# Chunked attention and a routed expert layer in one kernel: each batch's three slots in two phases, routing by batch

## The chip, the cores and the metric

The kernel runs on one core of one Trainium2 chip. The core has TensorE (matrix products and transposes; PE, with its weight loads as PEld), VectorE (DVE), ScalarE (ACT), GpSimd (POOL) and SyncE (SP), each with its own queue of instructions, and 16 DMA engines that all queues share. SBUF is the working memory with 128 partitions; PSUM is the memory that TensorE writes, in eight banks. The metric is the device time of one execution in microseconds (us), taken as the median of several runs. The profile is of one execution of its own.

## The reference

The input is four batches, eight heads, 768 positions and 64 values a head. Attention is by chunks of 32 queries: a chunk sees 8 memory keys, its own 32 positions, 16 to the left and 8 to the right, so 64 keys. Its output, 3072 tokens of 512 values, goes into a layer of 8 experts, two for each token, chosen by noisy logits.

```python
for c in range(nc):                                  # 24 chunks of 32 queries
    k_full = np.concatenate([mem_k, k_ctx], axis=2)  # 8 + up to 56 keys
    scores = scale * np.matmul(q_c, k_full.transpose(0, 1, 3, 2))
    a = np.exp(scores - np.max(scores, axis=-1, keepdims=True))
    a = a / (np.sum(a, axis=-1, keepdims=True) + 1e-09)
    out[:, :, c_start:c_end] = np.matmul(a, v_full)

logits = x @ w_gate
noisy_logits = logits + np.log1p(np.exp(x @ w_noise)) * noise
top2 = np.argpartition(-noisy_logits, 2, axis=1)[:, :2]
# top2_w: softmax over the two chosen logits
for e in range(E):
    for k in range(2):
        mask = top2[:, k] == e
        h = np.maximum(x[mask] @ w1[e], 0.0)
        out[mask] += top2_w[mask, k, None] * (h @ w2[e])
```

## The kernel before

**Two stages.** First attention with routing, then the experts. A token's pair of experts is one of 28; attention's rows are written to a DRAM table `xd`, and routing makes for each pair a list of up to 128 tokens, so that the expert stage gathers 128 rows of a pair at a time (L671), multiplies them by both experts' weights (L714, L726) and scatters the result (L677). The first gather needs all of routing.

**Slots.** A batch has 768 tokens: three slots (`TP` = 3) of 256, twelve slots (`NT`) in all. A slot goes through these steps, each a function:
- `scores` (L402): 40 small matmuls into PSUM `ps_s`, then on VectorE the row maximum (L423) and the subtraction into `sc` (L425).
- `exps` (L428): ScalarE's exponential into `pb`.
- `turn_p` (L433): eight 128x128 turns on TensorE into a PSUM bank, copied by ScalarE into `pT`.
- `values` (L442): row sums (L447) and products with the windows of v (L453) on TensorE into `ps_o`; on VectorE the reciprocals (L457) and two scalings (L460) into `xrow`.
- `turn_x` (L466): turns of the rows, copied by ScalarE into `xT`.
- `gate` (L475): logits of eight experts and eight noise columns, copied by VectorE into `lg_all`.

Ahead of a batch's first scores stand its `turns` (L546, `turn` L387): eight units, four of k and four of q, each with twelve turns on TensorE and two copies (k, L398) or one (q, L397). The turned keys are held once (`kT`), the turned queries twice (`qT`).

**Loads.** The inputs of a batch come by POOL's queue (`load_v`, `load_kq`, into two buffers `nat`), with a cast to bf16. POOL spreads v by heads (`spread_v`, L368); SP's queue writes it to DRAM, and POOL's queue reads it back in windows (`window_v`, L374 to L383) into one of two buffers `vb`. All of this, and the buffers of `xrow`, lies in the SBUF space of the weights of experts 2 to 7 (experts 0 and 1 hold none but small inputs), so the weights are loaded late: experts 0, 1 and 2 by `load_expert` in batch 2, the others during the expert stage.

**Routing.** `Route` holds a run of token groups of 128. Its steps are `noise` (two ScalarE operations, L247 and L248), `choose` (14 VectorE operations, L265 to L282, ending in the one-hot `ohp` of the pair), `weights` and `values` (POOL or VectorE), `order`, `ranks` (TensorE, L288 to L292), `settle` (VectorE, L317 to L335: ranks, totals, one-hot slots), `lists` (TensorE, L352, and an addition, L359), and at the end `decode` into gather indices (L490 to L498).

**What sets the order.** Under `manual_schedule` (L516) the program's order is the order on TensorE, ScalarE, VectorE and SP; on POOL the pinned instructions keep theirs. The loop over slots (L562) is a pipeline: in step i it issues the scores of slot i+1, the turns of slot i's probabilities, the row turns of slot i-1, the values of slot i, the exponentials of slot i+1 and the logits of slot i-1. The turns of the next batch stand in the middle slot of a batch (`PLAN`, L558; half of batch 2's and 3's query units one step earlier than the rest). Of k and q, q is loaded and turned first from batch 1 on. Routing is in four runs (L561): `r0` of 6 groups, `ra` of 8, `rb` of 6 and `rc` of 4, whose steps are spread over later slots; `rb` and `rc` are interleaved after the last slot (L624 to L654).

**PSUM.** `ps_s` has two banks, `ps_o` two, the small sums and logits one, and three banks in a ring (`bank`, L141) serve all turns, ranks and lists.

Of the kernel before, what the change touches and what calls it, by code (L numbers as in the profile page):

```python
# [11 lines left out]
F32 = mybir.dt.float32  # L12
# [10 lines left out]
def kernel(  # L23
# [96 lines left out]
        load_nat(vn, v, b)  # L120

    def load_kq(b):
        for x in ((1, 0) if b else (0, 1)):
            load_nat(nat[b % 2][x], (k, q)[x], b)

    load_v(0)
# [2 lines left out]
    actx = ExitStack()  # L129
    keep = actx.enter_context(tc.tile_pool(name="keep", bufs=1))  # L130
    work = actx.enter_context(tc.tile_pool(name="work", bufs=2))
    route = actx.enter_context(tc.tile_pool(name="route", bufs=1))
    psT = actx.enter_context(tc.psum_pool(name="psT", bufs=1))
    psS = actx.enter_context(tc.psum_pool(name="psS", bufs=1))
    psO = actx.enter_context(tc.psum_pool(name="psO", bufs=1))
    psG = actx.enter_context(tc.psum_pool(name="psG", bufs=1))


    ring = [0]

    def bank(shape, dtype, name):  # L141
        ring[0] += 1
        return psT.tile(shape, dtype, name=name, tag=f"ps_t{ring[0] % 3}")

    nc.scalar.preload_act_table_set("natural_log_exp_and_others")
    identb = const.tile([128, 128], BF16, name="identb")
# [254 lines left out]

    def scores(t):  # L402
        b, tp = divmod(t, TP)
        ps_s = psS.tile([128, 2, HP, 2, KW], F32, name="ps_s")
        for j in range(2):
            for pair in range(HP):
                tk = (2 * tp + j) * 128
                nc.tensor.matmul(out=ps_s[:, j, pair, :, 0:NM], lhsT=qT[b % 2][:, pair, tk:tk + 128],
                                 rhs=mkT[:, pair, :, b * NM:(b + 1) * NM], start=True, stop=True)
        for j in range(2):  # L410
            for pair in range(HP):
                tk = (2 * tp + j) * 128
# [12 lines left out]
        nc.vector.tensor_tensor(out=sc, in0=s3, in1=bc(mx, KW), op=Alu.subtract)  # L425
        return sc
# [6 lines left out]
    def turn_p(pb):  # L433
        p_p = bank([128, 2 * HP, 128], BF16, name="p_p")
        for x in range(2 * HP):
            nc.tensor.transpose(out=p_p[:, x, :], in_=pb[:, x].rearrange("p a w -> p (a w)"),  # L436
                                identity=identb)
        pT = work.tile([128, 2 * HP, 128], BF16, name="pT")
        nc.scalar.copy(pT, p_p)  # L439
        return pT  # L440

    def values(t, pT, between=None):  # L442
        b, tp = divmod(t, TP)
        ps_g = small[:, t % 2, 0:2 * H].rearrange("p (j h) -> p j h", j=2)
        for x in range(2 * HP):
            j, pair = divmod(x, HP)
            nc.tensor.matmul(out=ps_g[:, j, 2 * pair:2 * pair + 2], lhsT=pT[:, x, :], rhs=ones2,  # L447
                             start=True, stop=True)
        ps_o = psO.tile([128, 2, HP, 2, D], F32, name="ps_o")
        for j in range(2):  # L450
            for pair in range(HP):
                for r in range(4):
# [6 lines left out]
        for j in range(2):  # L459
            nc.vector.tensor_tensor(out=xr[:, j, 0:Dm].rearrange("p (h d) -> p h d", h=H),  # L460
                                    in0=ps_o[:, j].rearrange("p c a d -> p (c a) d"), in1=bc(rs[:, j], D), op=Alu.mult)
            if j == 0 and between is not None:
                between()
        return xr

    def turn_x(xr):  # L466
# [49 lines left out]
    with tc.manual_schedule(engines={ET.PE, ET.Activation, ET.DVE, ET.SP}):  # L516
# [16 lines left out]
        load_kq(1)  # L533
        spread_v(1)
        load_v(2)
        pbs[0] = exps(scores(0))
        nc.vector.tensor_copy(wgn, wgs)
        pf = work.tile([128, 2, NP], F32, name="pf")
        sidon(pf, pab)
        sidon(desc, desc)  # L540
        nc.vector.tensor_tensor(out=pcode, in0=pf[:, 0], in1=pf[:, 1], op=Alu.add)
        p_nz = bank([128, E, NG], F32, name="p_nz")
        for e in range(E):
            nc.tensor.transpose(out=p_nz[:, e], in_=nzr.rearrange("g (p e) -> g e p", e=E)[:, e], identity=identf)
        nc.vector.tensor_copy(nz.rearrange("p g e -> p e g"), p_nz)
        def turns(b, units):  # L546
            for u, eng in units:
                for o_, i_ in turn(b, u):
                    (nc.scalar.copy if eng else nc.vector.tensor_copy)(o_, i_)  # L549

        def fill(i, at):
            b, tp = divmod(i, TP)
            if b + 1 < B:
                turns(b + 1, PLAN[min(b, 1)].get((tp, at), ()))

        KS = ((0, 1), (1, 0), (2, 1), (3, 0))
        QS = ((4, 1), (5, 1), (6, 1), (7, 1))
        PLAN = ({(1, 2): QS + KS},  # L558
                {(1, 1): QS[0:2], (1, 2): QS[2:4] + KS})

        r0, ra, rb, rc = Route(0, 6, 8), Route(6, 8, 8), Route(14, 6, 8), Route(20, 4, 4)  # L561
        for i in range(NT):  # L562
            b, tp = divmod(i, TP)
            last = i == NT - 1
            more = b + 1 < B

            if tp == 0 and more:
                window_v(b + 1)
                if b + 2 < B:
                    load_kq(b + 2)  # L570
                    spread_v(b + 2)
                if b + 3 < B:
                    load_v(b + 3)
            if i in (2 * TP, 2 * TP + 1):
                load_expert(i - 2 * TP)
            fill(i, 0)
            if i == 2 * TP + 2:
                load_expert(2)
                ra.weights(nc.gpsimd)
                ra.order()  # L580
                ra.values(nc.gpsimd, 0, NV)
            if i == TP + 2:
                r0.weights(nc.gpsimd)
                r0.order()
                r0.values(nc.gpsimd, 0, NV)
            if not last:
                sc = scores(i + 1)

            pTs[i] = turn_p(pbs.pop(i))
            if last:  # L590
                keep_x(b, 0, SO - 2, nc.scalar)
            elif i and tp == 0:
                keep_x(b - 1, 0, SO, nc.scalar)
            if i:
                xTs_[i - 1] = turn_x(xrs.pop(i - 1))
            fill(i, 1)
            xrs[i] = values(i, pTs.pop(i), (lambda: gate(i - 1, xTs_.pop(i - 1))) if last else None)
            if last:
                break
            pbs[i + 1] = exps(sc)  # L600
            if i in (TP + 2, 2 * TP + 2):
                (ra if b > 1 else r0).ranks()
            if i:
                gate(i - 1, xTs_.pop(i - 1))
            if i in (TP + 2, 2 * TP + 2):
                advance((ra if b > 1 else r0).settle())
            if i in (2 * TP, 3 * TP):
                (ra if b > 2 else r0).lists(0, NV)
            if i == TP:
                r0.noise()  # L610
                chosen = r0.choose()
                advance(chosen, 8)
            if i == TP + 1:
                advance(chosen)
            if i == 2 * TP + 1:
                ra.noise()
                advance(ra.choose())
            if i == NT - 2:
                rb.noise()
                chosen = rb.choose()  # L620
                advance(chosen, 7)
            fill(i, 2)

        i = NT - 1  # L624
        keep_x(b, SO - 2, SO, nc.sync)
        xT = turn_x(xrs.pop(i))
        advance(chosen)
        rb.weights(nc.gpsimd)
        rb.values(nc.gpsimd, 0, 2)
        gate(i, xT)  # L630
        rc.noise()
        rb.ranks()
        advance(rb.total())
        chosen = rc.choose()
        advance(chosen, 4)
        advance(rb.place())
        advance(chosen)
        rc.weights(nc.gpsimd, 0, 2)
        rc.values(nc.gpsimd, 0, 2)
        rc.weights(nc.gpsimd, 2, 3)  # L640
        rc.ranks()
        rb.slots(nc.vector)
        rb.lists(0, 2, more=True)
        advance(rc.place())
        rc.slots(nc.vector, 2)
        rc.lists(0, 2, head=rb)
        src, dst = next(dec), next(dec)
        rb.order()
        rc.order()
        rb.values(nc.vector, 2, NV)  # L650
        rc.values(nc.vector, 2, NV)
        rb.lists(2, NV, more=True)
        rc.lists(2, NV, head=rb)
        next(dec)  # L654


# [329 lines left out]
```

## Time and profile before

| | us |
|---|---|
| median of 3 runs (lowest, highest) | 358.13 (357.63, 360.51) |
| profiled execution | 358.42 |
| its span, first to last instruction | 356.7 |
| first scores of batch 0 in PSUM | 24.95 |
| last logits copied (L482) | 129.14 |
| first gather of expert rows (L671) | 137.47 |
| TensorE busy from 150 to 340 | 188.89 of 190 |

The busy time of the whole span is 285.9 us on TensorE, 170.3 on VectorE, 136.9 on ScalarE and 134.3 on POOL, but these are sums over two stages with different limits. The times in the timeline count from the span's first instruction; the execution took 1.7 us more than its span. Lines such as L439 are lines of the kernel before.

### The profile page before, as it was taken

Reading aid. Unit: us, or ns where it says so; the run is one execution under the profiler, and the core shown is the slowest. Engines: PE = TensorE matmul, PEld = TensorE weight load, DVE = VectorE, ACT = ScalarE, POOL = GpSimd, SP = SyncE. Lnnn points to the kernel's source line nnn. Section 1 sums busy time; section 2 is a strip of 40 time slices with the busy share of each in tenths; the row PEclk is TensorE's granted clock in tenths of the full one; section 3 lists DMA queues with packets and bytes.
Section 4 is the critical chain, followed back from the end, with each engine's and each line's share of the span. In section 5 each row is a group of like instructions: output and inputs, shape, how many; then the busy total and the mean of one; then the engine's idle time right before and its main releaser. Section 6 shows DMA issues by size and latency. Waiting matters only on the chain.

```text
span 356.7 us, 7042 instructions
## 1 busy us (share of the span) xinstructions
PE 285.9 (80%) x2934; PEld 186.3 (52%) x2955; DVE 170.3 (48%) x349; ACT 136.9 (38%) x189; POOL 134.3 (38%) x181
## 2 busy tenths in 40 slices
PE   0356577777847732999999999999999999999991
PEld 0245455666736621865544465664455775565540
DVE  7656456699689885531133302954310334223221
ACT  8813645564645610144322343213243222243310
POOL 6460573354453036706530744332580122201122
PEclk9995655565687865699999999999999999999998
DMA  8999999999999999499999999961289971100012
GB/s 122 235 171 169 245 174 208 251 198 211 247 156 208 253 249 180 106 194 143 178 196 235 209 173 252 159 119 51 87 166 189 208 184 54 53 2 2 25 47 81
DMA packets 49866, 56.97 MB, mean 160 GB/s; under 512 B 16931, under 2 KB 39523, under 8 KB 49828
## 3 DMA queue, kind: packets, MB, share of 16 engines
q0 software_dynamic: 34240, 46.82, 73.2%
q1 hardware_dynamic: 13920, 6.62, 10.9%
q10 hardware_dynamic: 1668, 3.02, 2.4%
q8 instruction: 25, 0.41, 0.5%
q14 instruction: 13, 0.11, 0.1%
HBM read 70.39 MB, written 13.96 MB: 236 GB/s over the span
## 4 chain that ended last, share of the span: by engine, by line
PE 33%; issue 20%; POOL 5%; DVE 4%; DMA 3%; POOLq 1%; ACT 0%; DVEq 0%
PE p_h L714 18%; PE p_y L726 13%; POOL out_dram L677 4%; DMA out_dram<-y,main_dst 1%; DMA xTt<-xt 1%; DMA xt<-xd,main_src 1%; POOL xt L671 1%; DVE w_all L460 1%; PE p_xt L691 0%; POOL w_all L844 0%; POOLq L981 0%; DVE mx L423 0%; DVE sc L425 0%; ACT xT L472 0%; PE ps_o L453 0%
## 5 line engine op out<-in xcount | busy, mean ns | idle before, releaser
L714 PE MATMUL p_h<-xTt,w_all 128*128 128x256 bf16 (+3 forms) x669 | 102.7, 313 | 0.7 <-DVE xTt L692 0.5
L726 PE MATMUL p_y<-w_all,h 128*128 128x512 bf16 x446 | 102.3, 379 | 0.9
L714 PEld LDWEIGHTS <-w_all 128*128 128x128 bf16 x736 | 70.0, 101 | 36.3 <-issue 0.7
L702 ACT ACTIVATE h<-p_h 128x512 bf16<-128x512 f32 (+1 forms) x81 | 44.7, 551 | 95.9 <-PE p_h L714 88.3
L726 PEld LDWEIGHTS <-h 128*128 128x128 bf16 x464 | 45.3, 98 | 51.6
L700 DVE TENSOR_SCALAR h<-p_h 128x512 bf16<-128x512 f32 (+1 forms) x49 | 31.0, 633 | 82.8 <-PE p_h L714 73.7
L677 POOL DMA_INDIRECT out_dram<-y,main_dst x28 | 30.9, 1103 | 87.9 <-DVE y L732 75.4
L732 DVE SCALAR_TENSOR_TENSOR y<-p_y,main_w,y 128x512 f32<-128x512 f32 x28 | 21.0, 750 | 39.2 <-PE p_y L726 32.5
L393 PE MATMUL p_t<-identb,w_all 128*64 128x128 bf16 x384 | 20.6, 288 | 23.0 <-DMA w_all<-in_k_dram 13.4
L671 POOL DMA_INDIRECT xt<-xd,main_src x28 | 27.9, 997 | 24.2 <-DMA xTt<-xt 13.0
L730 ACT ACTIVATE y<-p_y,main_w 128x512 f32<-128x512 f32 x28 | 19.2, 687 | 37.0 <-PE p_y L726 36.0
L393 PEld LDWEIGHTS <-w_all 128*64 128x64 bf16 x384 | 18.1, 155 | 25.2 <-DMA w_all<-in_k_dram 13.9
L439 ACT COPY pT<-p_p 128x1024 bf16<-128x1024 bf16 x12 | 12.1, 1012 | 27.5 <-PE p_p L436 27.5
L383 POOL DMA_DIRECT2D w_all<-vd x16 | 11.8, 747 | 23.8 <-DMA vd<-vp 19.3
L460 DVE TENSOR_TENSOR w_all<-ps_o,rs 128x512 bf16<-128x512 f32 x24 | 15.6, 686 | 8.2 <-PE ps_o L453 7.8
L415 PE MATMUL ps_s<-kT,qT 128*32 128x112 bf16 x384 | 11.6, 276 | 7.2 <-DVE kT L549 5.4
L368 POOL COPY vp<-w_all 128x1536 bf16<-128x1536 bf16 x8 | 11.5, 1469 | 13.2 <-DMA w_all<-in_v_dram 13.2
L430 ACT ACTIVATE pb<-sc 128x1024 bf16<-128x1024 f32 x12 | 12.8, 1063 | 8.9 <-DVE sc L425 8.7
L549 DVE COPY kT<-p_t 64x768 bf16<-64x768 bf16 x12 | 11.5, 955 | 7.9 <-PE p_t L393 7.8
L425 DVE TENSOR_TENSOR sc<-ps_s,mx 128x1024 f32<-128x1024 f32 x12 | 14.7, 1225 | 0.8
L423 DVE TENSOR_REDUCE mx<-ps_s 128x16 f32<-128x1024 f32 x12 | 14.7, 1224 | 0.8 <-PE ps_s L415 0.5
L453 PE MATMUL ps_o<-w_all,pT 128*32 128x128 bf16 x384 | 10.9, 280 | 3.3 <-issue 2.0
(172 smaller groups left out, 284.0 us busy)
## 6 DMA issues: line engine op xcount, KB each, us to landing
w_all<-in_moe_w_dram POOLq DMA_DIRECT2D x16, 1024.0 KB, 20.7
w_all<-in_moe_w_dram POOLq DMA_DIRECT2D x8, 512.0 KB, 13.8
w_all<-in_v_dram POOLq DMA_DIRECT2D x4, 768.0 KB, 12.1
w_all<-in_k_dram POOLq DMA_DIRECT2D x4, 768.0 KB, 20.9
w_all<-in_q_dram POOLq DMA_DIRECT2D x4, 768.0 KB, 18.1
vd<-vp SPq DMA_DIRECT2D x4, 768.0 KB, 9.0
w_all<-vd POOLq DMA_DIRECT2D x8, 384.0 KB, 13.0
w_all<-vd POOLq DMA_DIRECT2D x8, 288.0 KB, 13.3
```

Source lines behind the costliest of these rows:

```text
L393: nc.tensor.transpose(out=p_t[own(par), s, :], in_=src[:, 2 * pair + par, s * D:(s + 1) * D], identity=identb, tile_position=(0, par * 64))
L423: nc.vector.tensor_reduce(out=mx, in_=s3, axis=AX, op=Alu.max)
L425: nc.vector.tensor_tensor(out=sc, in0=s3, in1=bc(mx, KW), op=Alu.subtract)
L460: nc.vector.tensor_tensor(out=xr[:, j, 0:Dm].rearrange("p (h d) -> p h d", h=H), in0=ps_o[:, j].rearrange("p c a d -> p (c a) d"), in1=bc( ...
L671: i = nc.gpsimd.indirect_dma_start(out=xts[key].bitcast(I32), out_offset=None, in_=xd, in_offset=bass.IndirectOffsetOnAxis(ap=ix, axis=0))
L677: i = nc.gpsimd.indirect_dma_start(out=out, out_offset=bass.IndirectOffsetOnAxis(ap=ix, axis=0), in_=y, in_offset=None, bounds_check=N - 1 ...
L700: nc.vector.tensor_scalar(out=out_, in0=in_, scalar1=0.0, scalar2=None, op0=Alu.max)
L702: nc.scalar.activation(out=out_, in_=in_, func=Act.Relu)
L714: nc.tensor.matmul(out=o, lhsT=w(kp * F + f * 128, 128), rhs=x[:, kp], start=(kp == 0), stop=(kp == KP - 1))
L726: nc.tensor.matmul(out=p, lhsT=h[:, (f * n + j) * 128:(f * n + j + 1) * 128], rhs=w(KP * F + f * Dm, Dm), start=(f == 0), stop=(f == FB - 1))
L730: nc.scalar.activation(out=y, in_=p, func=Act.Copy, scale=weight)
L732: nc.vector.scalar_tensor_tensor(out=y, in0=p, scalar=weight, in1=y, op0=Alu.mult, op1=Alu.add)
```

## The change

The loop over slots is replaced by a loop over batches. A batch is: its turns, the start of the next loads, `weigh` (scores, exponentials and turned probabilities of its three slots), the lists of the batch before, `mix` (values, row turns and logits of the three), and then its whole routing up to `settle`. The runs of routing are four of 6 groups, one for each batch. The small preparations after the first scores are now a function called between `weigh` and `mix` of batch 0. `ps_s` and `ps_o` share a ring of two buffers (`wide`), and `pT` gets three buffers. k is loaded ahead of q in every batch, and units 1 and 6 of a batch's turns are copied by VectorE, the rest by ScalarE. Expert 0 is loaded in batch 2, experts 1 and 2 in batch 3. `values` loses its hook between the two scalings. In batch 3 the turned probabilities of the last slot come after the values of the first, and the lists of batch 2 after the values of the last.

```diff
     def load_kq(b):
-        for x in ((1, 0) if b else (0, 1)):
+        for x in range(2):
...
+    deep = actx.enter_context(tc.tile_pool(name="deep", bufs=TP))
-    psS = actx.enter_context(tc.psum_pool(name="psS", bufs=1))
-    psO = actx.enter_context(tc.psum_pool(name="psO", bufs=1))
+    psB = actx.enter_context(tc.psum_pool(name="psB", bufs=1))
...
+    def wide(shape, name):
+        ring[1] += 1
+        return psB.tile(shape, F32, name=name, tag=f"ps_w{ring[1] % 2}")
...
-        ps_s = psS.tile([128, 2, HP, 2, KW], F32, name="ps_s")
+        ps_s = wide([128, 2, HP, 2, KW], "ps_s")
...
-        pT = work.tile([128, 2 * HP, 128], BF16, name="pT")
+        pT = deep.tile([128, 2 * HP, 128], BF16, name="pT")
...
-        ps_o = psO.tile([128, 2, HP, 2, D], F32, name="ps_o")
+        ps_o = wide([128, 2, HP, 2, D], "ps_o")
...
+        units = [(u, u not in (1, HP + 2)) for u in range(2 * HP)]
+
+        def weigh(b):
+            for j in range(TP):
+                if j < 2:
+                    sc_[j] = scores(b * TP + j)
+            for j in range(TP):
+                pbs[j] = exps(sc_.pop(j))
+                if b < B - 1 or j < TP - 1:
+                    pTs[j] = turn_p(pbs.pop(j))
+                if j + 2 < TP:
+                    sc_[j + 2] = scores(b * TP + j + 2)
+
+        def mix(b):
+            t = b * TP
+            for j in range(TP + 2):
+                if j < TP:
+                    xrs[j] = values(t + j, pTs.pop(j))
+                    if pbs:
+                        pTs[TP - 1] = turn_p(pbs.pop(TP - 1))
+                    if b == B - 1 and j == TP - 1:
+                        r[b - 1].lists(0, NV)
+                    if b == B - 1 and j:
+                        keep_x(b, 4 * j - 4, 2 * j + 2, nc.sync)
+                if 0 < j <= TP:
+                    xTs_[j - 1] = turn_x(xrs.pop(j - 1))
+                if j > 1:
+                    gate(t + j - 2, xTs_.pop(j - 2))
+            if b < B - 1:
+                keep_x(b, 0, SO, nc.scalar)
+
+        r = [Route(b * SO, SO, SO) for b in range(B)]
+        for b in range(B):
+            if b:
+                turns(b, units)
             if b + 1 < B:
                 window_v(b + 1)
+            if b + 2 < B:
+                load_kq(b + 2)
+                spread_v(b + 2)
+            if b + 3 < B:
+                load_v(b + 3)
+            if b == B - 2:
+                load_expert(0)
+            if b == B - 1:
+                load_expert(1)
                 load_expert(2)
+            weigh(b)
+            if b == 0:
+                settings()
+            elif b < B - 1:
+                r[b - 1].lists(0, NV)
+            mix(b)
+            if b < B - 1:
+                r_ = r[b]
+                r_.noise()
+                advance(r_.choose())
+                r_.weights(nc.gpsimd)
+                r_.order()
+                r_.values(nc.gpsimd, 0, NV)
+                r_.ranks()
+                advance(r_.settle())
+
+        rc = r[B - 1]
         rc.noise()
+        advance(rc.choose())
         rc.values(nc.gpsimd, 0, 2)
+        rc.weights(nc.gpsimd)
         rc.ranks()
         advance(rc.place())
         rc.slots(nc.vector, 2)
+        rc.lists(0, 2)
         src, dst = next(dec), next(dec)
         rc.order()
         rc.values(nc.vector, 2, NV)
+        rc.lists(2, NV)
         next(dec)
```

The loop over slots, `fill`, `PLAN` and the interleaved end of `rb` and `rc` go.

More of the change, by code (lines that the diff above doesn't have):

```diff
@@ L131 @@
     work = actx.enter_context(tc.tile_pool(name="work", bufs=2))
+    deep = actx.enter_context(tc.tile_pool(name="deep", bufs=TP))
     route = actx.enter_context(tc.tile_pool(name="route", bufs=1))
     psT = actx.enter_context(tc.psum_pool(name="psT", bufs=1))
-    psS = actx.enter_context(tc.psum_pool(name="psS", bufs=1))
-    psO = actx.enter_context(tc.psum_pool(name="psO", bufs=1))
+    psB = actx.enter_context(tc.psum_pool(name="psB", bufs=1))
     psG = actx.enter_context(tc.psum_pool(name="psG", bufs=1))
-    ring = [0]
+    ring = [0, 0]
     def bank(shape, dtype, name):
@@ L437, in turn_p, with values @@
                                 identity=identb)
-        pT = work.tile([128, 2 * HP, 128], BF16, name="pT")
+        pT = deep.tile([128, 2 * HP, 128], BF16, name="pT")
         nc.scalar.copy(pT, p_p)
         return pT
-    def values(t, pT, between=None):
+    def values(t, pT):
         b, tp = divmod(t, TP)
@@ L461, in values @@
                                     in0=ps_o[:, j].rearrange("p c a d -> p (c a) d"), in1=bc(rs[:, j], D), op=Alu.mult)
-            if j == 0 and between is not None:
-                between()
         return xr
@@ L535, with settings @@
         load_v(2)
[L536 to L545, printed above, removed]
+        def settings():
+            nc.vector.tensor_copy(wgn, wgs)
+            pf = work.tile([128, 2, NP], F32, name="pf")
+            sidon(pf, pab)
+            sidon(desc, desc)
+            nc.vector.tensor_tensor(out=pcode, in0=pf[:, 0], in1=pf[:, 1], op=Alu.add)
+            p_nz = bank([128, E, NG], F32, name="p_nz")
+            for e in range(E):
+                nc.tensor.transpose(out=p_nz[:, e], in_=nzr.rearrange("g (p e) -> g e p", e=E)[:, e], identity=identf)
+            nc.vector.tensor_copy(nz.rearrange("p g e -> p e g"), p_nz)
         def turns(b, units):
@@ L549, in turns @@
                     (nc.scalar.copy if eng else nc.vector.tensor_copy)(o_, i_)
-        def fill(i, at):
-            b, tp = divmod(i, TP)
-            if b + 1 < B:
[L554 to L567, printed above, removed]
-                window_v(b + 1)
[L569 to L577, printed above, removed]
-                load_expert(2)
[L579 to L630, printed above, removed]
-        rc.noise()
[L632 to L638, printed above, removed]
+        units = [(u, u not in (1, HP + 2)) for u in range(2 * HP)]
[9 more added lines that the diff above has]
+                    sc_[j + 2] = scores(b * TP + j + 2)
@@ new lines @@
+        sc_ = {}
+        r = [Route(b * SO, SO, SO) for b in range(B)]
+        for b in range(B):
+            if b:
+                turns(b, units)
+            if b + 1 < B:
+                window_v(b + 1)
+            if b + 2 < B:
[7 more added lines that the diff above has]
+                load_expert(1)
+                load_expert(2)
+            weigh(b)
[13 more added lines that the diff above has]
+                advance(r_.settle())
@@ L639 @@
+        rc = r[B - 1]
+        rc.noise()
+        advance(rc.choose())
         rc.values(nc.gpsimd, 0, 2)
-        rc.weights(nc.gpsimd, 2, 3)
+        rc.weights(nc.gpsimd)
         rc.ranks()
-        rb.slots(nc.vector)
-        rb.lists(0, 2, more=True)
         advance(rc.place())
         rc.slots(nc.vector, 2)
-        rc.lists(0, 2, head=rb)
+        rc.lists(0, 2)
         src, dst = next(dec), next(dec)
-        rb.order()
         rc.order()
-        rb.values(nc.vector, 2, NV)
         rc.values(nc.vector, 2, NV)
-        rb.lists(2, NV, more=True)
@@ L653 @@
-        rc.lists(2, NV, head=rb)
+        rc.lists(2, NV)
         next(dec)
```

## The prediction

> **What bounds the kernel now.** I read the profile in this order: the 40 slices, the busy time by stretch, the chain that ended last, the list of waits, and the order of time on each engine. The stretches first. Columns: stretch, length, busy us (instructions) of PE, PEld, DVE, ACT, POOL, then granted clock, DMA share, GB/s.
>
> ```profile
> 24.00:49.00 25.00, 15.06 (x335) 13.00 (x336) 13.46 (x23) 11.45 (x14) 9.94 (x12) 0.62 1.25 202
> 49.00:75.00 26.00, 19.03 (x399) 16.29 (x399) 18.39 (x39) 14.40 (x19) 10.50 (x12) 0.51 1.18 215
> 75.00:101.00 26.00, 19.39 (x423) 16.25 (x422) 22.12 (x41) 15.20 (x20) 14.06 (x20) 0.67 1.16 209
> 101.00:128.00 27.00, 17.59 (x413) 14.67 (x412) 23.54 (x50) 13.33 (x16) 6.14 (x13) 0.81 1.14 221
> 150.00:340.00 190.00, 188.89 (x1133) 107.69 (x1152) 59.30 (x114) 63.34 (x109) 60.64 (x61) 1.00 0.75 136
> ```
>
> The last line is the expert stage: TensorE is busy 188.89 of 190 us at full clock. The change does not touch it, so whatever it does before the first gather of expert rows (137.47 us in the timeline) moves the end by as much. The four lines above are the four batches of attention. No engine is full there (VectorE is nearest, 22.12 of 26), and the clock is granted at 0.51 to 0.81, so a batch is a chain of short steps handed from engine to engine. The waits between 26 and 130 us (total, times, longest):
>
> ```profile
> ACT pT L439 <- PE p_p L436: 27.5, 11, 4.8
> ACT pb L430 <- DVE sc L425: 8.7, 5, 4.5
> PE p_t L393 <- DMA w_all<-in_k_dram: 4.9, 2, 3.4
> PE p_t L393 <- DMA w_all<-in_q_dram: 4.2, 3, 2.6
> ```
>
> The loads cost TensorE 9.1 us in all. ScalarE's waits are slack so far, because between one slot's steps another slot's stand. The timelines give the prices:
>
> ```profile
> 26.51 1.23 DVE L425 TENSOR_TENSOR sc<-ps_s,mx 128x1024 f32<-128x1024 f32 x1
> 27.77 1.06 ACT L430 ACTIVATE pb<-sc 128x1024 bf16<-128x1024 f32 x1 [4.47 <-DVE sc L425]
> 28.98 1.03 PE L436 MATMUL p_p<-identb,pb 128*128 128x128 bf16 x8
> 30.05 1.01 ACT L439 COPY pT<-p_p 128x1024 bf16<-128x1024 bf16 x1 [1.22 <-PE p_p L436]
> 31.11 0.37 PE L447 MATMUL small<-ones,pT 128*128 128x2 bf16 x8 [1.10 <-ACT pT L439]
> 118.04 0.62 PE L436 MATMUL p_p<-identb,pb 128*128 128x128 bf16 x8
> 73.33 3.23 ACT L549 COPY kT<-p_t 64x768 bf16<-64x768 bf16 x4
> 73.31 0.33 DVE L282 TENSOR_TENSOR ohp<-pcode,pc 128x168 bf16<-128x168 f32 x1
> ```
>
> The reader sees one slot pass through four engines with 0.05 to 0.15 us between them, the same eight turns at 1.03 us under a half clock and 0.62 us at full clock, and four copies of turned keys in 3.23 us, 0.8 us each.
>
> **The change part by part.** On TensorE, ScalarE, VectorE and SP the written order is the executed order (batch 1's turns stand in the timeline exactly between the logits and scores where the program has them). So the new order can be priced as one chain. I take S, the moment when a batch's first scores are in PSUM (24.9 us for batch 0; nothing before it changes), and go from one S to the next at half clock.
>
> 1. Row maximum and subtraction of slot 0: memset 0.2, 1.26, 1.23, handover 0.05: **2.8**.
> 2. ScalarE's order is now exp 0, copy 0, exp 1, copy 1, exp 2, copy 2. The added wait is that exp 1 stands behind copy 0, which waits for TensorE's turns of slot 0. One round is 1.06 + 0.15 + 1.03 + 0.05 + 1.01, less 0.1 overlap of consecutive ScalarE rows: 3.2. VectorE would need only 2.5 a slot, so this loop decides, and the values of slot 0 stand behind the turns of slot 2 on TensorE. Two rounds, an exp and its turns: 6.4 + 1.06 + 0.15 + 1.0 = **8.6**; VectorE is idle meanwhile for some 3.5.
> 3. TensorE then runs the lists of the batch before (six matmuls, 1.00 in the row at 89.76, some 0.85 to the next; in batch 0 the noise turns, 1.06), the row sums 0.35 and the first products, 0.95: **2.1**. The settings' small VectorE work moved here lies in VectorE's idle time; without that cover it costs 1.3 once.
> 4. Scaling of slot 0 1.29, row turns of slot 0 1.0 (they precede the values of slot 2), values of slot 2 1.35, scaling 1.3 with handovers: **5.0**.
> 5. Second half of the last row turns 0.45, copy 1.0, logits 0.4, their copy 0.2: **2.1**. Storing the rows, moved to the batch's end, is an issue of 0.33 to 0.37 on ScalarE's queue that the trace shows beside a running copy: nothing.
> 6. Noise 0.55 and the choice. The choice's 14 operations took 1.9 (64.22 to 66.1) and 1.5 (72.16 to 73.64): **4.0**. In the kernel before this stood between slots; now TensorE has nothing else to do, since
> 7. the rank matmuls stand ahead of the next batch's turns: 0.82 (81.80 to 82.62), then the first unit's twelve turns 0.65: **1.5**.
> 8. Six of eight turn units are copied by ScalarE: three key units of two copies, three query units of one, nine copies of 0.8: **7.2**. VectorE's two units and its ranking (2.0, 84.60 to 86.63) fit beneath. Before, the turns stood beside another slot's work.
> 9. The scores still to do: **1.3**.
>
> The sum is 34.6 us a batch. At full clock the turns fall from 1.03 to 0.62, the products from 1.04 to 0.63, and so on through steps 2, 3, 4, 5, 7 and 9: 0.8 + 0.4 + 0.8 + 0.85 + 0.2 + 0.35 + 0.4 = 3.8 less, 30.8. The four stretches have a mean clock of 0.65, three tenths of the way from half to full; I take three tenths of 3.8 and get **33.5**, keeping both ends. In the last batch slot 2's turns follow slot 0's values and no lists stand ahead of them, so S to the last logits is 19.3 (18.7 with the same share; 17.2 at full clock). The routing after that, all six groups at once, is noise 0.6, choice 3.4, ranks 0.9, placing 0.65, slots 0.95, lists 0.6, addition 0.3, and 1.36 from the addition's end to the gather as now (136.11 to 137.47): 8.8, against 8.3 now (129.14 to 137.47).
>
> So the first gather comes at 24.9 + 3 x 33.5 + 18.7 + 8.8 = 152.9 instead of 137.5: 15.4 later. The profiled execution took 358.42 (span 356.7), 0.3 above the median of 358.13, so about **374**. All at half clock: 24.9 + 103.8 + 19.3 + 8.8 = 156.8, 378. All at full clock: 24.9 + 92.4 + 17.2 + 8.6 = 143.1, 364.
>
> Loads, windows: the turns of a batch come later than now (batch 1 at about 50; its k and q landed by 45.6 in the trace), so the 9.1 us of load waits vanish, as do the 3.3 that products waited, and what is late next is the chain above. On POOL's queue the window loads of batch 2 now stand behind the routing work of batch 0 (weights 1.6, values 1.9, waiting for the choice). They are issued about when they are now, 66, and needed at about 95. Nothing. One collision: the order comparison of batch 0 may run beside POOL's spreading of values, as in the row at 77.77, where it took 2.49 instead of 0.19; at worst that delays VectorE's turn units by 2.3 and the batch by 1.8, in the range.
>
> The clock deserves a look, since it is 3.8 us a batch. Columns: stretch, length, PE busy, granted clock, DMA share, GB/s.
>
> ```profile
> 54.00:56.00 2.00, 2.00 (x72) 0.50 1.13 170
> 56.00:58.00 2.00, 2.00 (x42) 0.50 1.14 104
> 102.00:104.00 2.00, 0.26 (x8) 1.00 1.04 193
> ```
>
> Four full microseconds did not raise it, and an almost idle stretch had it full. The Trainium skill, page "TensorE: Matmul & The Clock Gate", section "Part 1: The HAM clock gate (the 'warmup' mystery)", says that about 3.4 us of sustained work releases the full clock and an idle window of that length takes it back. By that rule the new order's dense run of values, row turns and logits would soon be at full clock and the wait for the choice would end it. The trace agrees only with a delay. If dense work kept the clock full throughout, the full-clock sum, 364, would hold; that is a rival below.
>
> **The rivals.**
>
> *Full clock throughout* (364). For it: steps 3 to 5 keep TensorE busy for about 8 us on end. Against it: steps 1, 2, 6 and 8 leave gaps, and 24 to 101 us ran at 0.51 to 0.67 with fewer gaps. Chance 0.14.
>
> *Faster: the VectorE bound.* If the waits in steps 2 and 6 to 8 were filled by other slots' and batches' work, a batch would be what VectorE needs, about 22.8 (22.12 and 23.54 in the two rows), and the gather would come at 24.9 + 68.4 + 18.7 + 8.8 = 120.8, time 342. The point of decision is a batch of 28.4, where 24.9 + 3P + 27.5 equals 137.5. For it: load waits vanish, and the last batch is shorter (27.5 from S to gather against 31 now, from 106.4). Against it: steps 6 to 8 alone are 12.7 in which TensorE can't go on, by written order. Chance 0.07 for clearly faster, 0.08 for a batch near 28.4 and no measurable change.
>
> *Slower still: late expert weights.* Experts 1 and 2 (4 MB) are now issued behind batch 2's routing on POOL, about 118 to 126, not at 99 to 105. In the trace 6 MB issued from 94 kept the DMA engines full until about 140; 4 MB at that rate take some 30 us, to 156, past the first gather at 152.9, whose rows then land late by 3 to 8: 377 to 382. Chance 0.11.
>
> *The change does not do what it says*, for instance phases that the scheduler mixes again, would give about the time before; the orders in the trace speak against it, and it is in the 0.08.
>
> **How the numbers follow.** The forecast with its neighbourhood (369 to 379) has 0.60. A measurement of this kernel can't tell less than about 1% from no change. Faster 0.07, the same 0.08, slower 0.85. The range takes in the full-clock case at 364 and most of the late weights: 363 to 381.
>
> **What would show it.** ScalarE's group of exps should wait for nothing but its place in the queue, with VectorE idle ahead of the reciprocals; TensorE should stand 4 us before each of three rank groups; nine ScalarE copies in a row should open batches 1 to 3; S should recur every 33 to 35 us; load waits of the turns should be gone from batch 1 on; the expert stage should stay 99% busy on TensorE and as long as now. The prediction is wrong if S recurs in under 30 us, or if TensorE waits for w_all loads after the first gather.

## The result and the profile after

The changed kernel takes 373.9 us (median of 4 runs, 373.28 to 375.69) against 358.45 for the kernel before beside it: a ratio of 1.043, 95% interval 1.037 to 1.049. The profiled execution took 373.76, its span 372.1. The forecast was 374, slower. Medians and ratios here and below leave out executions in a slower state of the chip.

The first gather of expert rows comes at 156.61 us instead of 137.47, 19.1 later. The first gather and the first expert matmul, in the kernel before and then in the new order:

```profile
137.47 1.61 POOL L671 DMA_INDIRECT xt<-xd,main_src  x1 [2.24 <-DVE facts L307]
144.14 1.86 PE L714 MATMUL p_h<-xTt,w_all 128*128 128x128 bf16 x16 [0.52 <-DVE xTt L692]
```

```profile
156.61 1.71 POOL L648 DMA_INDIRECT xt<-xd,main_src  x1 [1.58 <-DVE facts L311]
161.31 1.86 PE L691 MATMUL p_h<-xTt,w_all 128*128 128x128 bf16 x16 [0.52 <-DVE xTt L669]
```

The execution is only 15.3 longer, so what follows the gather gave 3.8 back.

The stretches of the new order, each from one batch's first scores in PSUM to the next one's; columns as before (length, busy us of PE, PEld, DVE, ACT, POOL, then granted clock, DMA share, GB/s):

```profile
24.90:59.70 34.80, 21.55 (x425) 18.14 (x426) 21.13 (x48) 16.59 (x20) 15.38 (x22) 0.79 1.21 198
59.70:95.90 36.20, 19.50 (x422) 16.31 (x423) 21.14 (x44) 16.59 (x20) 18.06 (x25) 0.64 1.21 223
95.90:130.20 34.30, 19.38 (x429) 16.33 (x426) 20.86 (x44) 16.59 (x20) 8.11 (x13) 0.65 0.92 164
165.00:355.00 190.00, 190.00 (x1160) 108.17 (x1158) 59.94 (x116) 62.90 (x108) 64.45 (x66) 1.00 0.73 138
```

From the first scores to the first gather the engines have about the work they had: TensorE 73.9 us (72.7 before), VectorE 81.7 (85.4), ScalarE 59.2 (55.3). It is spread over 131.7 us instead of 112.5, in batches of 34 to 36 us instead of 26 to 28. The expert stage is full as before.

The waits of TensorE between 26 and 155 us that bear on this (total, times, longest; `issue` stands where the profile shows nothing that ended the wait, called below a wait for nothing shown):

```profile
PE p_p L440 <- ACT pb L434: 22.1, 12, 2.8
PE p_rank L292 <- DVE ohp L286: 13.4, 3, 4.7
PE p_rank L292 <- DVE facts L311: 4.4, 1, 4.4
...
PE p_p L440 <- issue: 1.6, 1, 1.6
```

The first is the round of exponential, turns and copy (L434, L440, L443), the next two the choice that stands ahead of the ranks four times, 4.4 to 4.7 us each. No load stands in the full list; the 9.1 us of waits for k and q are gone. The chain that ended last, batch 2's part of it (start, length, what):

```profile
98.77 1.06 ACT pb L434
99.88 1.05 PE p_p L440 x8
100.95 1.01 ACT pT L443
101.96 0.97 ACT pb L434
...
115.17 0.37 PE small L482 x8
115.80 0.25 ACT ns L251
...
119.50 0.34 DVE ohp L286
119.89 0.32 PE p_rank L292
...
121.53 0.79 ACT kT L552
122.33 0.79 ACT kT L552
```

The chain goes through exponential, turns, copy, next exponential, and later from the logits through noise, choice and ranks into the copies of turned keys on ScalarE, as steps 2 and 6 to 8 had it.

### The profile page after: what moved, and what is told of

It reads as the page before. It is cut to its first block, busy times and chain, and to the rows that moved or that the text cites. A ratio compares the mean times of both kernels' runs of the same rounds, so it can differ in the third digit from the quotient of the medians.

```text
span 372.1 us, 7061 instructions
## 1 busy us (share of the span) xinstructions
PE 287.3 (77%) x2951; PEld 186.4 (50%) x2951; DVE 165.9 (45%) x346; ACT 140.8 (38%) x192; POOL 135.0 (36%) x181
## 4 chain that ended last, share of the span: by engine, by line
PE 43%; issue 21%; ACT 12%; DVE 11%; DMA 7%; POOL 4%; POOLq 1%; DVEq 0%; ACTq 0%
PE p_h L691 17%; PE p_y L703 13%; DMA w_all<-in_q_dram 4%; ACT kT L552 4%; POOL out_dram L654 3%; PE p_p L440 3%; ACT pb L434 3%; DVE w_all L464 2%; PE p_t L397 2%; ACT pT L443 2%; PE ps_o L457 2%; DVE mx L427 1%; DVE sc L429 1%; ACT xT L474 1%; DMA out_dram<-y,main_dst 1%
## 5 line engine op out<-in xcount | busy, mean ns | idle before, releaser
L703 PE MATMUL p_y<-w_all,h 128*128 128x512 bf16 x464 | 103.7, 379 | 0.0
L691 PEld LDWEIGHTS <-w_all 128*128 128x128 bf16 x736 | 69.2, 99 | 36.1 <-issue 0.7
L648 POOL DMA_INDIRECT xt<-xd,main_src x28 | 27.9, 997 | 22.5 <-DMA xTt<-xt 10.9
L397 PE MATMUL p_t<-identb,w_all 128*64 128x128 bf16 x384 | 22.1, 293 | 17.6 <-DMA w_all<-in_k_dram 8.4
L440 PE MATMUL p_p<-identb,pb 128*128 128x128 bf16 x96 | 12.6, 310 | 23.6 <-ACT pb L434 22.1
L397 PEld LDWEIGHTS <-w_all 128*64 128x64 bf16 x384 | 18.9, 158 | 20.1 <-DMA w_all<-in_k_dram 8.6
L440 PEld LDWEIGHTS <-pb 128*128 128x128 bf16 x96 | 9.2, 140 | 26.8 <-ACT pb L434 25.0
L552 ACT COPY kT<-p_t 64x768 bf16<-64x768 bf16 x18 | 14.3, 793 | 16.2 <-PE p_t L397 15.9
L434 ACT ACTIVATE pb<-sc 128x1024 bf16<-128x1024 f32 x12 | 12.7, 1058 | 17.0 <-DVE sc L429 17.0
L443 ACT COPY pT<-p_p 128x1024 bf16<-128x1024 bf16 x12 | 12.1, 1012 | 15.2 <-PE p_p L440 15.2
L474 ACT COPY xT<-p_x 128x1024 bf16<-128x1024 bf16 x12 | 12.0, 1012 | 14.4 <-PE p_x L472 14.4
## 6 DMA issues: line engine op xcount, KB each, us to landing
w_all<-vd POOLq DMA_DIRECT2D x8, 288.0 KB, 15.3
```

Of the source, the lines that this page charges most:

```text
L397: nc.tensor.transpose(out=p_t[own(par), s, :], in_=src[:, 2 * pair + par, s * D:(s + 1) * D], identity=identb, tile_position=(0, par * 64))
L434: nc.scalar.activation(out=pb.rearrange("p x a w -> p (x a) w"), in_=sc, func=Act.Exp, scale=scale)
L648: i = nc.gpsimd.indirect_dma_start(out=xts[key].bitcast(I32), out_offset=None, in_=xd, in_offset=bass.IndirectOffsetOnAxis(ap=ix, axis=0))
L691: nc.tensor.matmul(out=o, lhsT=w(kp * F + f * 128, 128), rhs=x[:, kp], start=(kp == 0), stop=(kp == KP - 1))
L703: nc.tensor.matmul(out=p, lhsT=h[:, (f * n + j) * 128:(f * n + j + 1) * 128], rhs=w(KP * F + f * Dm, Dm), start=(f == 0), stop=(f == FB - 1))
```

## The experiments

Ratios are to the kernel before on the same chip. Profiled times of different chips differ by some us, so steps are compared as distances inside one trace. "S to S" is the distance between first scores of consecutive batches.

### Routing out of the way of the turns

```diff
-            if b:
-                turns(b, units)          # at the start of a batch
...
+                turns(b + 1, units[:2])
                 advance(r_.choose())
+                turns(b + 1, units[2:])
...
-                r_.ranks()
-                advance(r_.settle())
+                if b and j == 1:          # in weigh, behind turn_p(1)
+                    r[b - 1].ranks()
+                    advance(r[b - 1].settle())
```

> The new order with one thing moved: the next batch's turns come right behind the noise, with the choice between VectorE's first unit and the rest, and the rank matmuls and their VectorE work go into the next batch's score phase, behind the turns of slot 1. If the batch is one serial chain (my theory), the choice and the ranks no longer stand ahead of the turns: from a batch's last logits to the next first scores 9.0 us instead of 14.4, less 0.4 for two later lists and 1.5 for ranking inside the last batch, about 14 in all; up to 3.8 of it may be given back where the first gather meets busier DMA engines. Time 360 to 364. If the loads hold the stage (rival: the DMA engines are at a share of 0.8 to 1.25 all through it), moving the choice gives nothing and turns wait for loads instead: 371 to 374.

Ratio 1.016 (1.006 to 1.025), so 2.7% of the kernel before, some 10 us, under the new order's 1.043. On the 358.45 of the kernel before that is 364, the upper end of what I expected. The first scores of batches 0 and 1:

```profile
24.52 0.94 PE L419 MATMUL ps_s<-kT,qT 128*32 128x112 bf16 x32
53.97 0.94 PE L419 MATMUL ps_s<-kT,qT 128*32 128x112 bf16 x32
```

S to S was 29.5, 32.6 and 33.9. The first is 5.4 under the new order's 34.8, as the price said. The second holds one operation of the choice at 2.28 us instead of 0.21 (below), the third a TensorE wait of 4.65 for nothing shown. With these taken off, and the like in the new order, the second and third are 3.9 and 5.0 shorter. The chain holds; no wait of TensorE for a load stands in this attention stage.

### Exponentials ahead of the copies

```diff
             t = b * TP
             sc_[0], sc_[1] = scores(t), scores(t + 1)
+            pbs[0] = exps(sc_.pop(0))
+            sc_[2] = scores(t + 2)
+            pbs[1] = exps(sc_.pop(1))
             for j in range(TP):
+                if j == 1:
+                    pbs[2] = exps(sc_.pop(2))
                 if b < B - 1 or j < TP - 1:
                     pTs[j] = turn_p(pbs.pop(j))
```

> The new order with the score phase reordered: the scores of slot 2 and the exponential of slot 1 go ahead of the turns and the copy of slot 0, the exponential of slot 2 ahead of the copy of slot 1. If the round of ScalarE and TensorE in step 2 is on the path at 3.1 us a slot, VectorE's 2.5 takes its place and each batch is 1.2 shorter, the last one too: 4 x 1.2 = 4.8, time 369, and up to 1 more or less at the gather. If VectorE or the loads held the phase already, nothing: 373 to 374.

Ratio 1.046 (1.035 to 1.056): a miss. In the trace batches 0 and 2 are 1.0 and 1.1 shorter once the waits for nothing shown are taken off (33.8; 34.6 less 1.46), and the way from the last first scores to the gather is 0.9 shorter (25.5 against 26.4). What the edit saved was lost elsewhere: waits for nothing shown of 3.17 and 1.46 in attention and 2.33 in the expert stage, against 1.55 and none there in the new order's trace. Batch 1 holds the wait of 3.17 and an operation of the choice at 2.37 instead of 0.21, so it gives no price. The kernel was run again beside the new order.

### Values of slot 0 ahead of the turns of slot 2

```diff
-                if b < B - 1 or j < TP - 1:
+                if j < TP - 1:
                     pTs[j] = turn_p(pbs.pop(j))
...
-                    if b == B - 1 and j == TP - 1:
+                    if b and j == TP - 1:
                         r[b - 1].lists(0, NV)
```

> The new order with batches 0 to 2 in the order of batch 3: the turned probabilities of slot 2 come behind the values of slot 0, and the lists of the batch before behind the values of slot 2. In the trace first scores to last logits took 19.8 us in batch 2 and 17.8 in batch 3. If that order is the difference, 2.0 us less in each of three batches: 368. If the difference was the clock of the last batch or the missing lists alone, under 1 in all: 373.

Ratio 1.047 (1.038 to 1.055): a miss too. In its trace an operation of the choice took 3.61 instead of 0.21, and two waits for nothing shown took 2.93 and 1.81; its second run, below, is read beside the new order.

### All three

The three edits together.

> The three reorderings together on the new order. If they are parts of one serial chain their gains add: a batch of 35.1 falls by 5.4 + 1.2 + 2.0 to 26.5, under the 28.4 at which the new order equals the kernel before; about 25 us less in all, of which up to 4 is given back at the gather: 349 to 353, below the kernel before. If the loads set a floor, the turns of batches 1 and 2 wait for k and q and the time stays at 358 or above.

Ratio 0.989 (0.980 to 0.997): below the kernel before, though not by as much as expected. S to S was 27.1, 30.2 (with a wait of 4.36 for nothing shown) and 26.5. The rival of the loads came in part: TensorE waits 2.30 for q of batch 1 (2.68 in the second run), where the new order waits for no load. The first gather comes at 135.68, 20.9 earlier than in the new order, but the first expert matmul follows it after 7.75 us instead of 4.70.

### The new order and the three on one chip

> The changed kernel itself, unaltered, as the measure for the three beside it on the same chip, since the ratios of the kernels with reordered scores (1.0455) and reordered values (1.0465) came from another chip than its own (1.043). 373 to 378, ratio 1.037 to 1.049.

> The kernel with the exponentials ahead once more. Its trace has each batch 1.0 to 1.1 shorter than the new order's once TensorE's waits for nothing shown are taken off (3.17 and 1.46 in its attention stage, 1.55 in the new order's). If the serial chain is right and those waits are chance between runs, 3 to 5 us below the new order beside it. If shortening the chain brings the waits on, so that they belong to the edit, no difference: within 2.

> The kernel with the values ahead once more. By the chain 2.0 in each of three batches, 6 below the new order beside it, or 3 to 6 with waits as in its first trace (2.93, 1.81 and 2.58 against 1.55). If the edit is worth nothing, within 2 of it.

> The kernel with all three reorderings once more, beside the new order: first ratio 0.9885 to the kernel before, so 19 us below the new order and 3 to 5 below the kernel before. If the first result was a matter of that chip, it comes out level with the kernel before, 0.995 to 1.005.

| | median us | ratio | 95% interval |
|---|---|---|---|
| new order | 380.19 | 1.049 | 1.043 to 1.055 |
| exponentials ahead | 379.47 | 1.045 | 1.040 to 1.051 |
| values ahead | 378.37 | 1.045 | 1.039 to 1.051 |
| all three | 359.35 | 0.992 | 0.988 to 0.996 |

The single edits gain 0.7 and 1.8 at the median, inside the intervals, so both expected gains were missed; all three gain 20.8, more than the single gains (some 10 for the routing) make together. For the exponentials the expectation gave a result within 2 to the reading that the shorter chain brings the waits on. That reading isn't refuted: S to S is 33.8, 36.5 and 33.2 against 34.1, 36.5 and 34.6, and the wait in batch 1 was 3.17 and 3.22 in this kernel's two traces, 1.55 and 2.00 in the new order's. Batch 1 also holds the collision described below (1.83 instead of 0.21) and a wait of 1.31 for k.

The trace of the values kernel shows where its 6 us went. S to S is 32.1, 37.7 and 33.5, against 34.1, 36.5 and 34.6 for the new order beside it. Take off the waits for nothing shown (none, 2.43, 1.82 against none, 2.0, 0.6) and the first operation of batch 1's choice (2.50 against 0.32): the gains are 2.0, 1.4 and 2.3, together 5.7 of the 6 expected. The price of the step was right by this account, which takes each wait as lying on the chain in full, and two other costs took it. One is the waits for nothing shown, 4.25 against 2.6. The other is a collision. VectorE's and POOL's order of time in the values kernel, by engine (start, length, operation):

```profile
79.56 2.50 DVE L269 TENSOR_TENSOR ns<-ns,nz 128x48 f32<-128x48 f32 x1 [0.58 <-ACT ns L252]
82.09 0.21 DVE L271 TENSOR_TENSOR ns<-ns,lg_all 128x48 f32<-128x48 f32 x1
```

```profile
79.11 2.88 POOL L372 COPY vp<-w_all 128x1536 bf16<-128x1536 bf16 x2
```

The multiplication of noise, 0.21 otherwise, lasts until POOL's spreading of batch 3's values is through (82.0). In the new order's first trace the choice came 2.3 later and met only the copy's last 0.4 (it took 0.50). By the Trainium skill, page "GPSIMD Engine Reference", section "8. Key points", POOL shares its SBUF interfaces with VectorE and contends with VectorE's instructions that have two SBUF inputs. The traces agree: 2.28 to 2.50 in three kernels against 0.21, and the operations held up elsewhere in the choice and the ranking (3.61 above, 2.22 below) read two tiles from SBUF too.

### Quiet DMA engines at the gather

```diff
                 load_expert(1)
-                load_expert(2)
...
         rc.values(nc.gpsimd, 0, 2)
+        load_expert(2)
         rc.weights(nc.gpsimd)
```

> The new order with the 2 MB load of expert 2's weights issued just ahead of the first gather, not at the start of batch 3. In the new kernel the first expert matmul came 4.7 us after the first gather's issue, before it 6.7, and the DMA engines stood at a share of about 0 then, against 0.4 to 1.1 before. If quiet DMA engines are the reason, the 2.0 comes back: 6.7 from gather to first expert matmul and 375 to 376. If the reason is another, the distance stays at 4.7 and the time at 374.

Ratio 1.066 (1.057 to 1.075), 1.7% above the new order's 1.049 on the same chip, some 6 us. From the gather's issue (156.79) to the first expert matmul (167.82) it took 11.0 us. Its DMA engines stood at a share of 1.09 from 156 to 168; in the new order the share is 0.18 from 156 to 161, and in the kernel before 0.78 from 137 to 144. The order of time on TensorE with the late load:

```profile
166.72 0.58 PE L668 MATMUL p_xt<-identb,xt 128*128 128x128 bf16 x4 [8.86 <-issue]
167.82 1.87 PE L691 MATMUL p_h<-xTt,w_all 128*128 128x128 bf16 x16 [0.51 <-DVE xTt L669]
```

The first turns of gathered rows wait 8.86, against 2.06 in the new order. So a load under way at the gather is a cause of the longer distance, and 2 MB of it cost 6.3, three times what I expected. Load and gather go by the same queue (POOL's), so whether the rows wait there or at the busy DMA engines is not shown. In all ten traces with that traffic over, the distance is 4.65 to 4.73; with it, 6.67 (the kernel before), 7.75 and 9.46 (all three) and 11.0.

### Filler for TensorE, with and without loads

```diff
+        def warm(n):
+            for _ in range(n):
+                nc.tensor.matmul(out=small[:, 1, 64:128], lhsT=identb, rhs=ones[:, 0:64], start=True, stop=True)
...
+            warm(36)          # behind the first two scores; warm(10) and warm(26) later in weigh
...
+                warm(60)
                 r_.ranks()
```

> The new order with filler matmuls (128x64, output read by nobody) in TensorE's waits: 36 behind the first two scores, 10 and 26 between the turned probabilities, 60 ahead of the ranks. By the Trainium skill, page TensorE: Matmul & The Clock Gate, section Part 1, sustained work brings the full clock. If that holds here, the steps on the path are at full-clock price, turns of probabilities 0.62 instead of 1.03, granted clock in the batches above 0.9: 3.4 us less in each of three batches and 1.5 in the last, 362. If dense work does not raise the clock, as the stretch from 52 to 72 us of the kernel before suggests, it stays at 0.5 to 0.7 and the time at 373 to 376.

Ratio 1.050 (1.042 to 1.058), against 1.049 for the new order on the same chip: no faster. S to S is 33.3, 38.9 and 37.2. TensorE's waits for nothing shown had grown:

```profile
65.20 0.28 PE L419 MATMUL ps_s<-kT,qT 128*32 128x112 bf16 x3 [6.03 <-issue]
77.73 0.46 PE L457 MATMUL ps_o<-w_all,pT 128*32 128x128 bf16 x19 [0.62 <-issue]
106.34 0.28 PE L419 MATMUL ps_s<-kT,qT 128*32 128x112 bf16 x2 [4.21 <-issue]
```

Without these the batches are 33.3, 32.3 and 33.0: 1.3 to 2.4 less than the new order's 34.8, 34.7 and 34.2 (0.8 to 2.3 less than in its trace on the same chip). The granted clock is 0.76, 0.74 and 0.77 (0.79, 0.64 and 0.65 in the new order, 0.65, 0.67 and 0.60 in its trace on the same chip), and the matmuls that turn the probabilities take 264 ns each instead of 310. So the denser work raised the clock, as the Trainium skill, page "TensorE: Matmul & The Clock Gate", section "Part 1: The HAM clock gate (the 'warmup' mystery)", says. The clock stayed under the 0.9 that I expected, the gain is half or less of the 3.4 expected of the full clock, and the waits cost more than it brought.

The waits come at fixed places of TensorE's program. Counted in the timeline, they stand at matmul 604 in eight traces, and at 667, 732, 988, 1113, 1240 and 1370 in these or others: 604 plus a multiple of 64, within 4 (some matmul records are missing). That suggested a wait for the instructions themselves, brought in blocks by DMA. The traces bear it out. Their DMA lists have a queue of the kind `instruction` (q8) whose packets of 16 KB number 25 in the new order and 29 with the filler's 468 more matmuls. At each of the 23 waits of over 0.4 us in the attention stages of all traces, one such packet ends 0.9 to 1.8 us before TensorE goes on. In the wait of 6.03, from 59.16 to 65.20, it runs from 62.05 to 63.70.

To see whether the loads make these packets late, the loads of q, k and v of batches 2 and 3 were left out. Batches 2 and 3 then compute on other data and the lists differ, so only the attention stage can be compared (ratios 1.043 with the filler, 1.044 without it):

```diff
             if b + 2 < B:
-                load_kq(b + 2)
                 spread_v(b + 2)
-            if b + 3 < B:
-                load_v(b + 3)
...
-        load_v(2)
```

> The kernel with filler matmuls, and without the loads of q, k and v of batches 2 and 3 (6 MB; those batches compute on the data of batches 0 and 1, so the output and the lists are others, and only the attention stage can be compared). Theory: TensorE's waits for nothing shown (6.03, 0.62 and 4.21 in the filler kernel, at its matmuls 734, 988 and 1372) are waits for its instructions, which come by DMA behind the loads. Then without loads in 58 to 115 they fall under 2 in all, and batches 1 and 2 take 32 to 34 us each instead of 38.9 and 37.2. If they are waits on something else in the program, they stay at 10.

In batch 1 the waits at the same places fell from 6.03 and 0.62 to 0.15 and 0.41, and the batch from 38.9 to 31.5:

```profile
62.64 0.28 PE L419 MATMUL ps_s<-kT,qT 128*32 128x112 bf16 x3 [0.15 <-issue]
...
103.27 0.28 PE L419 MATMUL ps_s<-kT,qT 128*32 128x112 bf16 x2 [5.22 <-issue]
```

The third did not go: 5.22 instead of 4.21, and batch 2 took 38.1. There the weights of expert 0 were being loaded; the DMA share was 1.06 from 99 to 103, and 0.46 from 62 to 66. So the waits go where loads are gone and stay where they run. Batch 0 took 36.6 instead of 33.3; there the spreading of values now fell on two operations of the choice (3.01 together instead of 0.50). My sum of under 2 was wrong, because I had counted only the input loads.

> The new order without the same loads. If the attention stage is the serial chain, only the 1.55 wait in batch 1 goes and the batches take 34.2 to 34.8 as now (first scores to first scores). If loads hold any of it, batches 1 and 2 shorten by more than 2.

S to S is 35.9, 34.2 and 34.2, and TensorE has no wait for nothing shown in the attention stage. Batch 1 lost its 1.55 and 0.5 more (0.3 of it the collision), batch 2 nothing. In batch 0 the spreading, no longer held by a load, ran into VectorE's ranking (the slots 2.22 instead of 0.95). So the input loads hold nothing of the new order but that one wait: the 34.2 us are the chain's own.

## Why the prediction was right, step by step

**The chain.** From the trace of batch 2 (95.94 to 130.16), the steps measured against their half-clock prices: step 1 2.8 (2.8 in the prediction), step 2 8.3 (8.6), step 3 2.1 (2.1), step 4 4.4 (5.0), step 5 2.2 (2.1), step 6 4.1 (4.0), step 7 1.7 (1.5), step 8 7.4 (7.2), step 9 1.2 (1.3). The sum is 34.2 against 34.6. Moving steps 6 and 7 aside took 5.4 off the first batch and 3.9 and 5.0 off the others; this shows in the time as well. The rounds of step 2 were worth 1.0 to 1.1 in the first run's batches 0 and 2 (0.3 and 1.4 in the second's) where I had 1.2, and the order of values and turns 5.7 over three batches where the two traces had 6. These two show in the traces once waits and collisions are taken off, and in the time only in the kernel with all three. That step 8 costs its 7.4 rests on the trace alone.

**The clock share was wrong.** I took three tenths of 3.8 off the 34.6, because the granted clock had a mean of 0.65. The mean came out as assumed, 0.64 to 0.79, but the full-clock time fell almost only into step 4: the turned probabilities ran at 1.03 in every batch, the ranks at half clock. An average clock says nothing of which rows on the path get it. The batches were 34.8, 36.2 and 34.2 (33 to 35 was the sign I named), together 4.8 more than 3 x 33.5. Of batch 1, 1.55 was a wait for nothing shown. The kernel before has such a wait at the same place, matmul 604 (2.03), and I had counted that among the product waits that vanish. Another 0.3 was the collision, which I had placed in another operation (the order comparison, which kept its 0.17).

**The last batch and its routing** were 17.85 and 8.6 against 18.7 and 8.8: 1.1 less.

**That the end moves by as much as the first gather was wrong** by 3.8. The first expert matmul came 4.70 after the gather instead of 6.67: 2.0. The late load shows that this distance depends on the loads under way at that moment. From there to the last expert matmul it took 204.39 instead of 205.38, and from there to the end 8.06 instead of 8.90. On the chip of its second trace the new order's own expert matmuls took 208.70, with waits of 1.97 and 1.49 among them, so those 1.8 us are no property of the order that I can claim.

So the two misses, plus 3.7 at the gather and minus 3.8 behind it, cancelled. The direction and the mechanism were right; the closeness of 374 to 373.9 was luck to the extent of some 4 us.

**The rivals.** Full clock throughout fell: the granted clock was 0.64 to 0.79, and even the filler reached only 0.77. The VectorE bound fell for this order, but the point of decision held: with batches of 27.1, 30.2 and 26.5, together 83.8 where three times 28.4 makes 85.2, the kernel with all three edits comes out just below the kernel before. Late weights fell: the weights of experts 1 and 2, issued from 122 to 129, were in before the gather (DMA share 1.00 from 130 to 150, 0.08 from 155 to 160). That a late load hurts is shown by the run with one. Loads left the turns, as predicted, and the loads of windows held nothing; TensorE waits for k or q again only in kernels with a shorter chain (2.30 and 2.68 with all three edits, 1.31 in the second run with the exponentials ahead). The phases stayed apart, as the chain's order shows, so the change did what it says.

**Open.** Why the waits at fixed matmuls vary from 0.4 to 6.0 at the same traffic was not tried, nor whether a shorter chain brings them on. Waits of 1.8 to 2.7 us ahead of the third group of expert matmuls in eight traces don't fit this reading, and their cause stays open: they stand at a DMA share of 0.26 to 0.40, and around the one at 167.77 in the filler kernel without input loads no instruction packet runs between 149.1 and 174.1.

## What to carry to other kernels

When independent work is regrouped into phases, add up the chain that remains inside one phase, queue by queue: a copy that waits for another engine holds back everything behind it on its queue, and a step that used to stand between others' work (here choice and ranks, 3.9 to 5.4 a batch) becomes time. Price on-path matmuls by the clock in their own rows, not by the mean clock of the stretch. And look at what a shifted stage meets on arrival: the same gather took 4.7 or 11 us to its first matmul by the loads under way at that moment, and the same multiplication 0.2 or 2.5 by what POOL was copying.

## What was not expected of the hardware

TensorE stands still for 0.4 to 6.0 us at places of its program 64 matmuls (or multiples) apart, and goes on 0.9 to 1.8 us after a 16 KB packet of instructions has come in. In the attention stage this happened at DMA shares of 1.03 to 1.35, but for one wait of 0.41 at 0.26. With 468 more matmuls (447 in the records) the waits in attention were 10.9 us, against 1.55 and 2.6 in the new order's two traces. The kernel before has two such waits (2.03 and 1.12) itself.
